# A new hand-out order for 959 planned operations, with the DMA queue chosen per transfer

## The chip, the cores and the metric

The kernel runs on one core of a Trainium2 chip. What counts is the device time of one execution in microseconds (us). The core has a matrix engine (PE, TensorE), a vector engine (DVE), an activation engine (ACT, ScalarE), a general engine (POOL, GpSimd) and a queue engine that only issues transfers (SP, SyncE). Transfers (DMA) can be issued from SP or from ACT; each engine works through its own list in order.

## The reference

Three stages follow each other, all in float32. (1) Linear attention with a decay per head: 2 batches, 8 heads, 768 positions, head size 64; `out = (q k^T * decay) v + q state`, with the state carried from block to block. (2) A dense layer: `x` (1536 x 512), `h = x @ w_in` (512 x 2048), `g = h * clip(h + 3, 0, 6) / 6`, `y = g @ w_out`. (3) A soft mixture of 8 experts: `logits = y @ phi` (32 slots); a softmax over all 1536 tokens mixes `y` into 32 slots; each expert runs `relu(slots @ w1) @ w2` (512 x 1024 x 512); a softmax over the slots mixes the experts' outputs back to 1536 x 512.

## The kernel before, in words

The sequence is cut into 12 pieces of 128 tokens (t = 0 to 11, six pairs tp). For a piece, attention is: transposes of q and k (`f_tr`, `f_tk`), scores (`f_sc`), decay (`f_pm`), state (`f_kd`, `f_pv`, `f_st`) and output (`f_px`). The decay table `dec` is loaded back from a small table that the kernel stores first (`store_pw`, `load_dec`). The dense layer is cut into 48 units `h_unit(t, n)` (n = 0 to 3, a quarter of w_in), each in two halves of six matmuls (L915): 96 halves in all, which serve below as a ruler along PE's list. After a unit, ACT (`f_u`, L929) and DVE (`f_g`, L935) make g, and both must be done before its PSUM buffer is free for a later unit. w_in is split into a high and a low part (`split_w_in`: ACT and DVE, some on POOL), which lets the three matmuls per tile stand for one float32 product.

`y` is never formed: phi is multiplied into w_out (`make_w2s`, giving `w2s`), and g into that (`f_lg`, L1019). Both need a blockwise transposition across partitions: DVE transposes 32 x 32 blocks (`f_blocks` L996, `f_wb` L670), and a *move* of four DMAs of 128 KB from SBUF to SBUF (`f_move` L1006 for g, `f_wq` L683 for w_out) brings the blocks to their partitions. For tp = 0 to 4 g goes this way, 5 x 4 = 20 moves; the last pair is transposed on PE. The softmax over tokens runs pair by pair (`f_lr`, `f_exp`, `f_pd`); after the last, the slots are formed (`f_psi`, L1312), spread for the experts (`f_sim`), and the experts' products follow (`f_p1` L1439, `f_po` L1473), then the outputs (`f_pt`, `f_ot`, `f_out`).

Expert weights (64 loads `e`) and the stored w_out (8 loads `wo`), 72 loads of 512 KB, are read on SP into a ring of 50 buffers of 4 KB per partition that everything shares, so a load waits until its buffer is given back.

The order of all this is written out by hand: `ORDER` names the 959 operations by the place at which the kernel creates them. `Plan.run` goes through it with a cost in ns for each operation, so as to know which ring buffer is free first, and thereby gives each operation its buffers; then it emits the operations. Before, it emits them sorted by the modelled start `t0`; a DMA's queue is fixed by kind: loads, stores of w_out (`sto`) and `f_wq` on SP (`mwq='SP'`), `f_move` on ACT (`mvq='ACT'`), the output stores in turn on SP and ACT (7 and 5). At the very start PE runs `lamq_products` and then `f_first`, eight products of a zero tile (`blank`), which compute nothing that is used.

Of the kernel before, what the change touches and what calls it, by code (L numbers as in the profile page):

```python
# [135 lines left out]
class Plan:  # L136
# [19 lines left out]

    def op(
        self, eng, cost, fn, deps=(), prio=0.0, take=(), rel=(), dma=0, reserve=None, follow=None,
        mode="F", lag=None, extra=0, share=2,
    ):  # L160
        o = Op()
        o.extra, o.share = extra, share
        o.lag = lag
        o.follow = follow
# [1458 lines left out]
```

## Time and profile before

| | |
|---|---|
| device time, median of 3 runs | 312.93 us (312.2 to 314.39) |
| profiled execution | 310.75 us, of it 309.0 us span |
| PE busy | 279.3 us (90%) |
| DVE busy | 195.8 us (63%) |
| ACT busy (issuing DMAs not counted) | 121.1 us (39%) |
| POOL busy | 38.0 us (12%) |
| DMA | 85.99 MB, mean 278 GB/s |

The span runs from the first to the last instruction; the rest of the profiled time lies around it. "Busy" leaves out waiting and the issuing of transfers. The granted clock of PE has two levels, 2.4 GHz (1.0) and 1.2 GHz (0.5). The median of the runs lies 2.18 us over the profiled execution.

### The profile page before, as it was taken

How to read it: one execution, taken by the hardware profiler on the slowest of the kernel's cores; microseconds unless marked ns; L12 is line 12 of the kernel's file. 1: busy time of each engine (PE TensorE's matmuls, PEld its weight loads, DVE VectorE, ACT ScalarE, POOL GpSimd, SP SyncE). 2: the span in 40 equal slices, each digit the busy share in tenths (PEclk: the TensorE clock that was granted, in tenths of full speed). 3: DMA queues.
4: the chain of work that ended last, by engine and by line, in shares of the span. 5: the costliest groups of instructions: out<-in, count | busy, mean ns of one | idle time of the engine just before them, and what ended most of it. 6: DMA issues, size and time to landing. Idle time of an engine off the chain costs nothing.

```text
span 309.0 us, 7097 instructions
## 1 busy us (share of the span) xinstructions
PE 279.3 (90%) x2854; PEld 215.9 (70%) x2854; DVE 195.8 (63%) x319; ACT 121.1 (39%) x227; POOL 38.0 (12%) x53
## 2 busy tenths in 40 slices
PE   4899999998999978999896999998999997889892
PEld 3877888786878856876775586865888655556671
DVE  5299979999989737778766659175464242430242
ACT  2566786997862530311303222221223520201141
POOL 5215013242400020002020020000000001000000
PEclk9999999999999995999999999999999999999996
DMA  7999999947799868585764579896998999999988
GB/s 183 295 330 290 337 323 359 299 149 229 222 276 284 255 190 214 158 232 164 200 157 117 137 240 297 259 319 223 366 395 286 369 421 416 418 417 415 350 274 265
DMA packets 80480, 85.99 MB, mean 278 GB/s; under 512 B 42040, under 2 KB 67136, under 8 KB 80448
## 3 DMA queue, kind: packets, MB, share of 16 engines
q1 hardware_dynamic: 67056, 73.75, 72.4%
q10 hardware_dynamic: 13392, 11.80, 13.3%
q8 instruction: 22, 0.36, 0.4%
q14 instruction: 10, 0.08, 0.1%
HBM read 64.55 MB, written 7.35 MB: 233 GB/s over the span
## 4 chain that ended last, share of the span: by engine, by line
PE 43%; DMA 18%; DVE 13%; ACT 9%; ACTq 7%; issue 4%; SPq 2%; POOL 1%; POOLq 0%; DVEq 0%
PE h L915 22%; DMA e<-in_moe_w_dram 12%; ACTq L1006 7%; PE pd L1134 3%; DMA gq<-gb 3%; PE lg L1019 3%; DMA wq<-wb 3%; ACT g L929 2%; DVE tmp_i L543 2%; DVE pm L797 2%; DVE tmp_i L550 1%; DVE g L935 1%; PE px L825 1%; ACT whi L576 1%; PE px L820 1%
## 5 line engine op out<-in xcount | busy, mean ns | idle before, releaser
L915 PE MATMUL h<-whi,x 128*128 128x512 f32 x384 | 122.9, 401 | 5.4 <-DVE g L935 4.8
L915 PEld LDWEIGHTS h<-whi,x 128*128 128x128 f32 x384 | 71.5, 191 | 24.9 <-DVE g L935 6.3
L915 PE MATMUL h<-wlo,x 128*128 128x512 f32 x192 | 75.7, 394 | 0.0
L929 ACT ACTIVATE g<-h,half_b 128x512 f32<-128x512 f32 x48 | 32.9, 689 | 70.8 <-PE h L915 39.9
L935 DVE SCALAR_TENSOR_TENSOR g<-g,h 128x512 f32<-128x512 f32 x48 | 32.6, 680 | 29.7 <-ACT g L929 29.3
L996 DVE STREAM_TRANSPOSE gb<-g 128x1024 f32<-128x1024 f32 x20 | 40.4, 2026 | 3.2 <-DMA gq<-gb 2.4
L915 PEld LDWEIGHTS h<-wlo,x 128*128 128x128 f32 x192 | 36.5, 190 | 8.0
L769 ACT COPY tr<-pt 128x512 f32<-128x512 f32 x24 | 13.3, 586 | 22.7 <-DMA gq<-gb 7.3
L843 POOL TENSOR_TENSOR states<-states,lamq 64x256 f32<-64x256 f32 x16 | 10.6, 660 | 65.9 <-DVE states L856 57.1
L778 POOL TENSOR_TENSOR vd<-qk,dec 128x512 f32<-128x512 f32 x10 | 11.4, 1145 | 57.6 <-DVE wo_f L550 25.9
L1439 PE MATMUL p<-e,sim 128*32 128x256 f32 x256 | 15.0, 380 | 3.4 <-DMA e<-in_moe_w_dram 2.1
L1473 PE MATMUL po<-e,ht 128*32 128x128 f32 (+1 forms) x384 | 16.1, 309 | 1.1 <-DMA e<-in_moe_w_dram 1.1
L797 DVE TENSOR_TENSOR pm<-ps,dec 128x512 f32<-128x512 f32 x24 | 15.6, 680 | 0.9 <-PE ps L789 0.7
L670 DVE STREAM_TRANSPOSE wb<-wo_f 128x1024 f32<-128x1024 f32 x6 | 12.1, 2012 | 6.2 <-DMA wq<-wb 6.2
L1458 DVE STREAM_TRANSPOSE ht<-hsi 128x256 f32<-128x256 f32 x8 | 4.9, 635 | 17.2 <-ACT hsi L1450 17.2
L789 PE MATMUL ps<-tr 64*128 64x128 f32 x192 | 14.5, 285 | 1.3 <-ACT tr L769 0.9
L550 DVE SCALAR_TENSOR_TENSOR tmp_i<-tmp_i 128x512 int32<-128x512 int32 x16 | 12.3, 780 | 5.1 <-ACT tmp_i L536 4.4
L789 PEld LDWEIGHTS ps<-tr 64*128 64x128 f32 x192 | 12.1, 187 | 4.9 <-issue 1.9
L1473 PEld LDWEIGHTS po<-e,ht 128*32 128x32 f32 x384 | 11.5, 110 | 5.3 <-DMA e<-in_moe_w_dram 1.6
L1439 PEld LDWEIGHTS p<-e,sim 128*32 128x32 f32 x256 | 8.0, 110 | 9.2 <-DMA e<-in_moe_w_dram 3.1
L832 ACT CAST x<-px 128x512 fp32r<-128x512 f32 x12 | 7.0, 585 | 18.3 <-DMA gq<-gb 8.7
L579 POOL TENSOR_TENSOR wlo<-tmp_i,whi 128x512 fp32r<-128x512 f32 x8 | 10.7, 1353 | 23.1 <-ACT whi L576 23.1
(117 smaller groups left out, 366.3 us busy)
## 6 DMA issues: line engine op xcount, KB each, us to landing
e<-in_moe_w_dram SPq DMA_DIRECT2D x64, 512.0 KB, 8.2
gq<-gb ACTq DMA_DIRECT2D x80, 128.0 KB, 3.4
wraw<-in_moe_w_in_dram SPq DMA_DIRECT2D x16, 512.0 KB, 5.8
wo_raw<-in_moe_w_out_dram SPq DMA_DIRECT2D x16, 512.0 KB, 5.4
wo_d<-wo_f SPq DMA_DIRECT2D x32, 128.0 KB, 3.2
wo<-wo_d SPq DMA_DIRECT2D x8, 512.0 KB, 6.9
qk<-in_k_dram SPq DMA_DIRECT2D x12, 256.0 KB, 5.8
qk<-in_q_dram SPq DMA_DIRECT2D x12, 256.0 KB, 4.7
```

The lines of the kernel that those rows point to most:

```text
L550: DVE.scalar_tensor_tensor(out=lw if dst is None else dst(), in0=hp, scalar=3, in1=lw, op0=ALU.logical_shift_left, op1=ALU.bitwise_or,)
L670: DVE.transpose(out=x.rearrange("p q d c f -> p c d q f"), in_=y.rearrange("p c (d t q) -> p c d q t", d=KT, q=4),)
L769: ACT.copy(T["tr", t][:, i], T["pt", t, i])
L789: PE.matmul(ps[g][:, p], lhsT=y[r, 1, p], rhs=y[r, 0, p], start=True, stop=True)
L797: DVE.tensor_tensor(out=T["pm", t].rearrange("p (a g) c -> p g a c", g=2)[:, g], in0=T["ps", t][g], in1=T["dec"].rearrange("p (a g) c -> p ...
L915: PE.matmul(ph, lhsT=xt[:, a, kt], rhs=T[w, n, part][:, kt % 2], start=i == 0, stop=i == 3 * KT - 1,)
L929: ACT.activation(T["g", tp, n][:, i], T["h", t, n], AF.Relu, bias=half_b, scale=1.0 / 6.0)
L935: DVE.scalar_tensor_tensor(out=to, in0=to, scalar=1.0, in1=T.pop(("h", t, n)), op0=ALU.min, op1=ALU.mult,)
L996: DVE.transpose(out=x.rearrange("p q c i t -> p i c q t"), in_=T["g", tp, n].rearrange("p i (c t q) -> p i c q t", c=4, q=4),)
L1006: QUEUE[CFG["mvq"]].dma_start(out=y[:, a].rearrange("p c i t -> p (c i t)"), in_=x[32 * a : 32 * a + 32].rearrange("f q c i t -> f (q c i ...
L1439: PE.matmul(p1[32 * j : 32 * j + 32], lhsT=T["sim"][:, e, b4], rhs=T["e1", e, b4][:, 256 * j : 256 * j + 256], start=b4 == 0, stop=b4 == 3,)
L1473: PE.matmul(T["po", hf][32 * qd : 32 * qd + 32], lhsT=T["ht", e // 4][:, e % 4, b8], rhs=T["e2", e, b8 // 2][:, b8 % 2, lo:hi] if e < WHOL ...
```

## The change

The list is replaced by another order of the same 959 operations; nothing is computed differently. Read through the operations' names, the two lists differ as follows where the prediction needs it ("at 42" is after 42 of the 96 halves on PE's list):

| on PE's list, or on a queue | before | after |
|---|---|---|
| first on PE | `lamq_products`, `f_first`, then piece 0's transposes | `f_first`, `lamq_products`, then piece 1's transposes |
| first loads on SP | w_in, k of pieces 1 and 0, `store_pw`, q 0, w_in, q 1, `dec` | k and q of piece 1, w_in, k 0, `store_pw`, q 0, w_in, q 2, `dec` |
| `f_sums` of n = 2, 3, 0 | at 26, 42, 46 | at 42, 42, 48 |
| `f_lg` of pairs 0, 1, 2 | at 52, 56, 64 | at 52 to 54, 60, 64 |
| `f_lg` of pair 3 | two at 68, two at 74 | all at 74 |
| `f_lg` of pair 4 | one at 78, three at 96 | two at 80, two at 96 |
| expert and wo loads listed ahead of `f_psi` | 46 | 45 |
| expert loads listed within the first 18 halves | none | two |
| g moves on ACT / on SP | 20 / 0 | 7 / 13 |
| most g moves on ACT with nothing between them | 3 (pair 2) | 1 (once with a store right behind it) |

Twelve operations in `BY_ACT` go to ACT, the other operations marked `free` to SP: of the 46 free ones these are seven g moves (402 is the store of w_out 13, 415 a `f_wq` of n = 0, 910, 934 and 955 are output stores). On SP's new list the moves of pairs 3 and 4 (n = 1, 3 and n = 0, 1, 3) stand between expert loads. `f_first` must now be done before `lamq_products`. The cost numbers of the model change, a move or load is modelled in its parts, and a part starts in the model only when the part eight before it has landed (`lanes`). Emission follows `ORDER` itself.

```diff
 ORDER = (
-    0, 74, 11, 256, 75, 4, 73, 3, 1, 5, 6, 76, 77, 78, 258, 257, 259, 10, 7, 89,
...
+    0, 1, 73, 74, 75, 4, 7, 89, 91, 10, 3, 92, 5, 6, 9, 14, 8, 2, 15, 90,
...
 )
+BY_ACT = (402, 415, 633, 639, 653, 679, 693, 699, 719, 910, 934, 955,)
...
-        dma_free, side, mode, shared = 0, 0, "F", 0
+        dma_free, side, mode, shared, lanes = 0, 0, "F", 0, [(0, 0)] * 8
...
             o = self.ops[i]
+            if o.free:
+                o.eng = "ACT" if i in BY_ACT else "SP"
...
+            for _ in range(o.parts):
+                now = max(now, lanes.pop(0)[0])
+                for t, _ in sorted(lanes):
+                    if o.rows / o.parts + sum(n for x, n in lanes if x - 900 > now) <= 200:
+                        break
+                    now = max(now, t - 900)
...
+                lanes.append((o.t1, o.rows / o.parts))
+                now += cost / o.parts
+                o.te = now
...
-        for i in sorted(ORDER, key=lambda i: self.ops[i].t0):
-            self.slots = self.ops[i].slots
+        for i in ORDER:
+            self.slots, self.eng = self.ops[i].slots, self.ops[i].eng
             self.ops[i].fn()
...
-    op("PE", 430 * CFG["fill"]["first"], f_first, [], -3000, take=[b_h], rel=[b_h])
+    ops["first"] = op("PE", 430 * CFG["fill"]["first"], f_first, [], -3000, take=[b_h], rel=[b_h])
...
-    ops["lamq_p"] = op("PE", 1150, lamq_products, deps=[pw_done], prio=-9, take=[b_x], rel=[b_pw])
+    ops["lamq_p"] = op("PE", 1700, lamq_products, deps=[pw_done, ops["first"]], prio=-9, take=[b_x], rel=[b_pw])
...
-                SP.dma_start(out=wo_d[c2, q4, n], in_=x[32 * q4 : 32 * q4 + 32])
+                QUEUE[plan.eng].dma_start(out=wo_d[c2, q4, n], in_=x[32 * q4 : 32 * q4 + 32])
...
-                    QUEUE[CFG["mwq"]].dma_start(
+                    QUEUE[plan.eng].dma_start(
...
-                QUEUE[CFG["mvq"]].dma_start(
+                QUEUE[plan.eng].dma_start(
...
-                (ACT if j % 2 else SP).dma_start(
+                QUEUE[plan.eng].dma_start(
```

## Rows read from the trace of the kernel before

**Rows 1.** The page, sections 1 and 2: busy time, and PE's clock in 40 slices

```profile
PE 279.3 (90%) x2854; PEld 215.9 (70%) x2854; DVE 195.8 (63%) x319; ACT 121.1 (39%) x227; POOL 38.0 (12%) x53
...
PEclk9999999999999995999999999999999999999996
```

**Rows 2.** Stretches: length, busy of PE, PEld, DVE, ACT, POOL, clock, DMA share, GB/s

```profile
15.00:105.00 90.00, 86.47 (x739) 71.69 (x738) 84.56 (x131) 66.35 (x113) 21.45 (x21) 1.00 0.90 282
105.00:165.00 60.00, 52.73 (x477) 41.03 (x476) 41.22 (x43) 12.97 (x22) 6.85 (x9) 0.94 0.71 188
165.00:240.00 75.00, 73.54 (x568) 55.08 (x567) 42.62 (x68) 19.44 (x41) 2.30 (x3) 1.00 0.82 266
240.00:299.00 59.00, 53.18 (x978) 35.83 (x978) 19.16 (x58) 14.26 (x37) 0.96 (x1) 1.00 1.00 387
```

**Rows 3.** Waits of PE, 105 to 256 us: total us, times, longest

```profile
PE h L915 <- DVE g L935: 3.2, 2, 2.5
PE w2p L695 <- DMA wq<-wb: 3.0, 2, 2.6
PE lg L1019 <- DMA gq<-gb: 1.5, 1, 1.5
PE lg L1019 <- ACT sm L1078: 1.0, 1, 1.0
```

**Rows 4.** Chain of waits, 129 to 216 us, shares by line

```profile
by line: PE h L915 26.3%; ACTq L1006 25.2%; DMA gq<-gb 8.5%; PE pd L1134 7.8%; PE lg L1019 7.5%; issue 2.7%; PE ps L789 2.5%; PE px L825 2.5%; DVE gb L996 2.3%; PE pv L810 2.1%; PE px L820 2.1%; PE pt L752 2.0%; PE lr L1089 2.0%; ACT g L929
```

**Rows 5.** Chain of waits, 250 to 309 us: shares by line, and one piece

```profile
by line: DMA e<-in_moe_w_dram 63.4%; PE pt L1542 5.2%; PE po L1473 5.0%; PE pd L1134 4.0%; PE keep_on L493 3.3%; PE p L1439 2.7%; PE psi L1312 1.6%; ACT ot L1557 1.0%; PE lg L1019 0.8%; PE pc L1408 0.8%; PE lr L1089 0.7%; ACT sm L1078 0.6%;
...
256.51 0.96 PE psi L1312 x33
```

**Rows 6.** PE's timeline at the start: start us, us, instruction, [idle before]

```profile
4.61 2.04 PE L481 MATMUL lamq_p<-pw,selp 32*128 32x128 f32 x8 [4.61 <-POOL low_rows L347]
6.58 3.78 PE L498 MATMUL first<-acc 128*128 128x128 f32 x16
...
18.03 1.09 PE L825 MATMUL px<-pm,vd 128*64 128x128 f32 x16
```

**Rows 7.** Timelines of DVE and POOL at the start

```profile
0.83 0.17 DVE L303 MEMSET acc<- 128x128 f32 x1 [0.83 <-PEq L1608]
...
13.06 2.08 POOL L778 TENSOR_TENSOR vd<-qk,dec 128x512 f32<-128x512 f32 x2 [7.45 <-DMA dec<-pw_d]
```

**Rows 8.** PE's timeline: its longest wait after the start

```profile
116.30 0.74 PE L695 MATMUL w2p<-wq,phi_b 128*32 128x64 f32 x4 [2.58 <-DMA wq<-wb]
```

**Rows 9.** Chain pieces: 24 matmuls of the dense layer, ahead of and behind that first wait

```profile
89.00 5.72 PE h L915 x24
...
118.49 7.75 PE h L915 x24
```

**Rows 10.** ACT's timeline ahead of PE's wait of 2.5 us for g

```profile
154.17 8.47 ACTq L1006 DMA_DIRECT2D gq<-gb  x12
162.68 0.58 ACT L832 CAST x<-px 128x512 fp32r<-128x512 f32 x1 [8.68 <-DMA gq<-gb]
```

**Rows 11.** The page, section 6: DMA issues, KB each, median us to landing

```profile
gq<-gb ACTq DMA_DIRECT2D x80, 128.0 KB, 3.4
...
wq<-wb SPq DMA_DIRECT2D x24, 128.0 KB, 2.6
```

**Rows 12.** DMA issues, 165 to 240 us

```profile
e<-in_moe_w_dram SPq DMA_DIRECT2D x26, 512.0 KB, 5.7
gq<-gb ACTq DMA_DIRECT2D x33, 128.0 KB, 4.6
```

**Rows 13.** Waits of SP's queue over the run: total us, times, longest

```profile
SPq L391 <- DMA gq<-gb: 24.3, 7, 15.6
```

**Rows 14.** Issue of moves on either queue: duration ns min/median/max, first and last start

```profile
L1006 ACTq DMA_DIRECT2D gq<-gb x80: 550/622/1651, 109.4 to 233.3; - x80
...
L683 SPq DMA_DIRECT2D wq<-wb x24: 542/604/1310, 79.9 to 125.4; - x24
```

More of the change, by code (lines that the diff above doesn't have):

```diff
@@ L158, in op @@
         self, eng, cost, fn, deps=(), prio=0.0, take=(), rel=(), dma=0, reserve=None, follow=None,
-        mode="F", lag=None, extra=0, share=2,
+        mode="F", lag=None, extra=0, share=2, parts=0, rows=8, free=False,
     ):
         o = Op()
-        o.extra, o.share = extra, share
+        o.extra, o.share, o.parts, o.rows, o.free = extra, share, parts, rows, free
         o.lag = lag
@@ L209, in run @@
                 shared = now + cost
-            o.t0, o.te, done[e] = now, now + cost, now + cost + o.extra
-            if o.dma and e == "ACT":
-                at = max(side, now + 400)
-                side = at + o.dma * (o.share if dma_free > at else 1)
-                dma_free = max(dma_free, at) + o.dma
-                o.t1 = side + self.DMA_TAIL
-            elif o.dma:
-                dma_free = max(dma_free, now + self.DMA_LEAD) + o.dma
-                o.t1 = dma_free + self.DMA_TAIL
-            else:
-                o.t1 = o.te + self.SETTLE[e]
+            o.t0, o.te = now, now + cost
+            o.t1 = o.te + self.SETTLE.get(e, 0)
+            for _ in range(o.parts):
[4 more added lines that the diff above has]
+                    now = max(now, t - 900)
+                if e == "ACT":
+                    at = max(side, now + self.DMA_LEAD)
+                    by = max(0, dma_free - at)
+                    size = o.dma / o.parts
+                    side = at + min(o.share * size, by + max(0, size - by / o.share))
+                    dma_free = max(dma_free, at) + size
+                    o.t1 = side + self.DMA_TAIL
+                else:
+                    dma_free = max(dma_free, now + self.DMA_LEAD) + o.dma / o.parts
+                    o.t1 = dma_free + self.DMA_TAIL
+                lanes.append((o.t1, o.rows / o.parts))
+                now += cost / o.parts
+                o.te = now
+            done[e] = o.te + o.extra
             for b in o.rel:
@@ L361, in load @@
     def load(
-        fn, nbytes, deps=(), take=(), rel=(), n=1, prio=None, reserve=None, eff=1.0, lag=None, eng="SP",
+        fn, nbytes, deps=(), take=(), rel=(), n=1, prio=None, reserve=None, eff=1.0, lag=None, eng="SP", share=2, each=440, rows=8, free=False,
     ):
         o = op(
-            eng, n * plan.DMA_ISSUE, fn, deps=deps, prio=-1000 if prio is None else prio,
+            eng, n * each, fn, deps=deps, prio=-1000 if prio is None else prio, share=share, parts=n, rows=rows, free=free,
             take=take, rel=rel, dma=nbytes / 360 / eff, reserve=reserve, lag=lag,
@@ L399, in load_qkv @@
         ops["ld" + x, t] = load(
-            fn, KB512 / 2, take=take, rel=[] if take else [bufs[name, t]], eff=0.61,
+            fn, KB512 / 2, take=take, rel=[] if take else [bufs[name, t]], eff=0.81, rows=64,
             reserve=load_reserve,
@@ L414, in load_w_in @@
         ops["ldw", n, kt] = load(
-            fn, KB512, take=[ring_buf(("wraw", n, kt))], reserve=load_reserve, eff=1.08
+            fn, KB512, take=[ring_buf(("wraw", n, kt))], reserve=load_reserve, eff=1.16
         )
@@ L426, in load_wo_raw @@
         ops["ldo", kk] = load(
-            fn, KB512, take=[ring_buf(("wo_raw", kk))], reserve=load_reserve, eff=1.08
+            fn, KB512, take=[ring_buf(("wo_raw", kk))], reserve=load_reserve, eff=1.16
         )
@@ L467, in attn_moe_softmoe_kernel @@
             ops["dec"] = load(
-                load_dec, KB512, deps=[ops["pw_d"]], take=[ring_buf("dec")], eff=0.5
+                load_dec, KB512, deps=[ops["pw_d"]], take=[ring_buf("dec")], eff=0.85, rows=64
             )
@@ L625, in convert_wo @@
                 store, KB512, [ops["cwo", kk], ops["cwo", kk - 1]],
-                rel=[bufs["wo_f", kk // 2]], n=4, prio=CFG["sto"], eff=0.7,
+                rel=[bufs["wo_f", kk // 2]], n=4, prio=CFG["sto"], eff=0.7, each=470, share=4, rows=8, free=True,
             )
@@ L707, in make_w2s @@
                 done.append(load(
-                    f_wq(h), KB512, [o], take=[b_t[h]], rel=[b_wb], n=4, eff=0.9, eng=CFG["mwq"],
+                    f_wq(h), KB512, [o], take=[b_t[h]], rel=[b_wb], n=4, eff=0.95, eng=CFG["mwq"], each=640, share=5, rows=32, free=True,
                     prio=CFG["mw"] if CFG["mwq"] == "SP" else prio - 1,
@@ L856, in f_st @@
                     DVE.tensor_tensor(out=dst, in0=dst, in1=T["pv", t][r], op=ALU.add)
-        tq = op("PE", 350, f_tr(0), [ops["ldq", t]], prio, take=[b_q], rel=[b_qk])
+        tq = op("PE", 425, f_tr(0), [ops["ldq", t]], prio, take=[b_q], rel=[b_qk])
         eq = op(
@@ L868, in attention @@
         tk = op(
-            "PE", 350, f_tk, [ops["ldk", t], tq], prio, take=[b_k] + x_k["take"], rel=[b_qk] + x_k["rel"],
+            "PE", 435, f_tk, [ops["ldk", t], tq], prio, take=[b_k] + x_k["take"], rel=[b_qk] + x_k["rel"],
             extra=x_k.get("extra", 0),
@@ L873, in attention @@
         ek = op("ACT", 480, f_ev(1), [tk, eq], prio, rel=[b_k])
-        sc = op("PE", 1090, f_sc, [eq, ek], prio, take=[b_s], rel=[b_tr], mode="T")
+        sc = op("PE", 1000, f_sc, [eq, ek], prio, take=[b_s], rel=[b_tr], mode="T")
         ops["sc", t] = sc
@@ L880, in attention @@
             kd = op(
-                "POOL", 1010, f_kd, [ops["ldk", t], ops["ldv", t], ops["dec"]], prio,
-                rel=[b_qk, bufs["dec"]],
+                "POOL", 1060, f_kd, [ops["ldk", t], ops["dec"], ops["ldv", t] if GREEDY else None], prio,
+                rel=[b_qk, b_vd, bufs["dec"]],
             )
@@ L885, in attention @@
                 sm = op(
-                    "POOL", 1160, f_sm, [prev, ops["px", t - 1], ops["lamq"], zeros], prio,
+                    "POOL", 1390, f_sm, [prev, ops["px", t - 1], ops["lamq"], zeros], prio,
                     rel=[bufs["lamq"]],
@@ L892, in attention @@
         px = op(
-            "PE", 1030 if c == 0 else 1920, f_px, [pm1, ops["ldv", t], trd, prev], prio - 0.1,
+            "PE", 940 if c == 0 else 1960, f_px, [pm1, ops["ldv", t], trd, prev], prio - 0.1,
             take=[b_x], rel=[b_vd, b_pm, b_states] + ([b_trd] if c > 0 else []),
@@ L1038, in logits @@
                 [o] + ([lgs[-CFG["depth"]] if len(lgs) >= CFG["depth"] else None] + w2s_all if GREEDY else []),
-                take=[b_last], rel=[b_gb], n=4, eff=0.9, eng=CFG["mvq"],
+                take=[b_last], rel=[b_gb], n=4, eff=1.0, eng=CFG["mvq"], each=660, share=5, rows=32, free=True,
                 prio=CFG["mv"] if CFG["mvq"] == "SP" else prio - CFG["mva"],
@@ L1055, in logits @@
         ops["lg", tp, n] = ops["lg"] = op(
-            "PE", 520, f_lg, [o, w2s_all[n], ops.get("lg") if GREEDY or not opens else None],
+            "PE", 440, f_lg, [o, w2s_all[n], ops.get("lg") if GREEDY or not opens else None],
             prio - 0.5,
@@ L1204, in attn_moe_softmoe_kernel, with load_b @@
     bprio = [100.0]
-    def load_b(key, fn, take, eff=1.15, nbytes=KB512):
+    def load_b(key, fn, take, eff=1.13, nbytes=KB512, rows=8):
         bprio[0] += 1
@@ L1209, in load_b @@
             fn, nbytes, [ops["ldv", NT - 1]] if GREEDY else [], take=take, prio=bprio[0], reserve=pre_reserve,
-            eff=eff, lag=CFG["lag"],
+            eff=eff, lag=CFG["lag"], rows=rows,
         )
@@ L1351, in attn_moe_softmoe_kernel @@
         o = op(
-            "PE", 872, f_psi(i), [o, ant[i // 2], ops["wo", 2 * i], ops["wo", 2 * i + 1]], 55,
+            "PE", 930, f_psi(i), [o, ant[i // 2], ops["wo", 2 * i], ops["wo", 2 * i + 1]], 55,
             take=[] if i else [b_x], mode="T",
@@ L1581, in combine @@
             ot[j].append(op(
-                "ACT" if g % 2 else "DVE", 550 if W < 512 else 600, f_ot(g), [o] + ot[j], pr,
+                "ACT" if g % 2 else "DVE", 610, f_ot(g), [o] + ot[j], pr,
                 take=[] if i else [b_o], rel=[b_h],
@@ L1587, in combine @@
                     f_out(j), 512 * NO * W, ot[j], rel=[b_o], prio=pr if j % 2 else 99,
-                    eff=0.95, eng="ACT" if j % 2 else "SP",
+                    eff=1.0, rows=16, free=True, eng="ACT" if j % 2 else "SP",
                 )
```

10 lines of the change are left out of this document (5 added, 5 removed), and 94 rows, old and new, of the table ORDER.

## The prediction

> **What bounds the kernel now.** I read the page first: PE is busy 279.3 of 309.0 us [rows 1], so an order can at most win the other 30 us, and PE's own work is the same afterwards. The stretches tell where those 30 us lie and what else is full there [rows 2]. From 15 to 105 us PE idles 90 - 86.5 = 3.5 us, and DVE is busy 84.6 of the 90: this part is nearly full on two engines. From 105 to 165 us PE idles 60 - 52.7 = 7.3 us with no engine full (DVE 41 of 60, DMA share 0.71): waits in a row of handovers, not throughput. From 165 to 240 us it idles 1.5 us. From 240 to 299 us the DMA share is 1.00 at 387 GB/s. The rest is the start: PE does nothing until 4.61 us [rows 6].
>
> Then the waits of PE from 105 to 256 us, four lines: 3.2 + 3.0 + 1.5 + 1.0 = 8.7 us [rows 3]. Who makes them is told by the chain of waits over 129 to 216 us: 25.2% of it, 22 us of 87, is ACT issuing the DMAs of the g moves at L1006, and 8.5% their flight [rows 4]. One DMA holds ACT 0.62 us, so 80 of them hold it 50 us [rows 14]. The place to look at is 154.17 us: twelve issues in a row, 8.47 us, and the copy of x behind them has waited 8.68 us [rows 10]; from there it goes on over DVE to the PE wait of 2.5 us for g [rows 3].
>
> The end hangs on transfers: of the chain from 250 us on, 63.4% is the flight of expert weights [rows 5]. Slots are formed at 256.51 us, and the list has 72 - 46 = 26 of the 72 loads still behind that point. At the rate of the stretch a load takes 524,288 B / 387 GB/s = 1.35 us [rows 2], 35 us for 26, and eight or so in flight come on top: the tail is a fixed length of DMA, counted from `f_psi`. So the time falls by as much as `f_psi` comes earlier, provided the loads keep their place in relation to PE.
>
> **The change part by part.** The sum is made on the profiled execution, 310.75 us (span 309.0); the median of the runs is 2.18 us above it, and I shift the sum by that.
>
> *Zero products first.* They need only the blank tile, cleared at 1.00 us [rows 7], and take 3.78 us [rows 6]; now they stand behind `lamq_products`, which begins at 4.61 us. In the new order they lie inside that idle time: `lamq_products` ends at 6.65 us as before, and the transposes, which now begin when the zero products end, may begin up to 3.7 us earlier. What is late next is the decay table: POOL's first use of it waits until 13.06 us [rows 7], and the new list puts one more load of 256 KB ahead of it (0.93 us at 282 GB/s [rows 2]), so about 14.0 us. The first output product stands at 18.03 us now [rows 6], 5 us behind the table; DVE's new list does the two decay products ahead of the first low part of w_in (`f_lo`), the old one behind it, so the distance shrinks, while the table comes later. I take -2.0, the middle; bounds -3.7 (all of it) and 0 (table or conversion holds it).
>
> *15 to 105 us.* DVE has 5.4 us of idle, PE 3.5 [rows 2]; reordering can't thin out their work. I take -0.5, between -2.9 (most of PE's idle gone) and +2.5: two expert loads now come within the first 18 halves, where the DMA share is 0.90, and may push the conversion loads back by 2 x 1.35 us.
>
> *The sums of w2s.* `f_sums` of n = 2 moves from 26 to 42 on PE's list, that of n = 3 stays at 42 behind it, n = 0 goes from 46 to 48. The waits on `wq` are 3.0 us [rows 3]. Behind the long one of 2.58 us [rows 8] PE's clock stands at the half level: the clock of its slice is 0.5 [rows 1], and 24 matmuls take 7.75 us where 24 before took 5.72 [rows 9], which is 2.0 us. With three sums close together and more slack ahead of the first, I take all of it, -5.0; bounds -5.0 and 0, since n = 3 has not been given more room.
>
> *Moves off ACT.* Thirteen of 20 go to SP; one `wq` move and one store come to ACT, so ACT loses (52 - 8) x 0.62 = 27 us of issuing, nearly all between 109 and 233 us [rows 14]. No more than one move stands before ACT's next copy (once with a store behind: 8 issues, 5 us), where it was three. The waits for g, 3.2 us [rows 3], go: -3.2, bounds -3.2 and 0. On SP, an issue is as long (0.60 us [rows 14]); the 52 issues there cost 31 us of a queue that mostly waits for buffers: 24.3 us in one line alone [rows 13]. While SP waits for a block to be transposed, the loads behind it wait too.
>
> These rows say the gain lies in ACT's time. The Trainium skill says as much against any other gain: "DMA: Bandwidth & Descriptors", section "Issuing engines are not separate DMA queues", holds that transfers of all issuing engines share the same 16 DMA engines and that spreading them saves only the time of issuing, which is usually small beside the DMA. The trace agrees on the first; on "small" it differs, four issues being 2.5 us beside 3.4 us to landing [rows 11, 14]. By the rule's "small" this term would be about zero and the time 3.2 us longer than mine.
>
> *New waits.* The logits keep their two waits, 1.5 and 1.0 us [rows 3], as I see no more room for them on balance (pair 1 goes from 56 to 60, but the second of pair 4 comes from 96 to 80). Some handover that is covered now will not be: I add the same again, +2.4. Bounds 0 and +5.2, twice the longest wait seen.
>
> *Tail.* 45 loads ahead of `f_psi` instead of 46, and the same five loads last: 0, bounds one load, 1.35 us, either way. Which engine issues the output stores, the new buffers and the model's cost numbers: 0, since the last stores are again two small ones on either queue, and buffers matter only through the waits counted above.
>
> Sum: -2.0 - 0.5 - 5.0 - 3.2 + 2.4 = -8.3 us. Nearly all of it lies ahead of 165 us, where the DMA has room (share 0.71); everything behind moves forward as it is. Profiled 302.4, median **304.6 us**. All bounds together: 16 us less, or 9 us more.
>
> **Rivals.** *The gain is taken back ahead of `f_psi`.* The start holds at the decay table, and the waits of the middle only change places: DVE is nearly full to 105 us, and four pairs of logits now come later, closer to each other. Against it: the middle has no full engine. Then -2.0 (start) -0.5 +1.0 or so: about 311.4, within 309.8 and 316.
>
> *SP's queue becomes the bound (slower).* Place: the moves of pairs 3 and 4, which now stand on SP between expert loads that wait for buffers. SP's longest wait is 15.6 us [rows 13]. If such a one lies ahead of a move, `f_lg` waits for it; a move at the right moment would have gone out from ACT. Behind two halves of cover (2 x 6 matmuls of 0.24 us, 2.9 us) some 12.7 us stay, plus 2.0 us for the half clock [rows 9]: -8.3 + 14.7 = +6.4, so 319.3 us. From a wait of 9.2 us on (8.3 + 2.9 - 2.0) the gain is gone, from 12.3 us on the kernel is slower by 1%. Also a move sent out behind loads lands later: loads take 5.7 us there, moves on their own queue 4.6 [rows 12], while `wq` on a quiet SP took 2.6 [rows 11]; that adds 1.1 us. Beside it, the Trainium skill ("DMA: Bandwidth & Descriptors", "Queues, rings and completion order") has each DMA engine take turns between the issuing queues' rows, which would favour a move on ACT's own row; no row here separates the two. For it: rows 13. Against it: two of pair 4's moves feed logits that stand at 96, with 16 halves of room, and from 240 us on (share 1.00) loads queue up anyway.
>
> *The change does not do what it says.* If the first matmul waits for something later than the blank tile, the zero products don't move into the idle time: 2.0 us more than mine, 306.6. It lies within the range.
>
> **Numbers.** A single comparison tells about 1% (3.1 us) from no change. The forecast case, own range 299.5 to 309.8: 0.62. More than that (a tail with fewer waits too): 0.05. The first rival: 0.18. The slower one: 0.15. Faster 0.67, same 0.18, slower 0.15. The range leaves 0.05 below and 0.15 above: 299.5 to 315.
>
> **What would show it.** Right: the first matmul at about 1 us and `px` of the first piece near 16 us (18.03 now); no slice of PE's clock below 1.0 between 20 and 290 us; ACT's issues at L1006 28 instead of 80, with no run of more than four, and their share of the chain from 129 to 216 us under a half of 25%; PE's idle time between 105 and 165 us under 4 us; `f_psi` near 248 us and 52 us from there to the end. Wrong: `f_psi` early but the tail longer than 55 us (loads held back on SP); waits of `f_lg` on `gq` of more than 4 us in sum; or new PE waits before 105 us of more than 4 us.

## The result and the profile after

The new kernel takes 298.87 us (median of 4 runs, 298.24 to 299.67); the kernel before, run beside it, 313.66 us (312.2 to 323.22). The ratio is 0.9544, 95% interval 0.9492 to 0.9597. The direction was forecast, the size was not: 304.6 us lies 5.7 us too high, and the time is 0.6 us below the range's low end. Here and below the ratios leave out runs in which the chip was in a slower state (over 1.5% above the kernel's fastest), the medians have them in, and the profile of e1 is of such a run.

The profiled execution of the new kernel took 299.16 us (span 297.4), against 310.75 (309.0). So from profile to profile 11.6 us went, where the sum had 8.3. The other 2.5 us of the miss are no event in the kernel: I added 2.18 us for the distance from profile to median, and the new kernel's profiled run stands 0.3 us above its median instead of 2.18 below.

The page of the new kernel, sections 1 and 2, answers to [rows 1]:

```profile
PE 275.9 (93%) x2854; PEld 213.3 (72%) x2854; DVE 195.7 (66%) x319; ACT 121.0 (41%) x227; POOL 38.1 (13%) x53
...
PEclk9999999999999999999999999999999996999998
```

The low clock slice in the middle is gone, and there is another one at 245 us, in the tail. Busy time of the other engines is the same. The stretches of [rows 2] in the new kernel (same columns):

```profile
15.00:105.00 90.00, 86.58 (x677) 71.30 (x672) 79.76 (x125) 66.04 (x113) 22.08 (x21) 1.00 0.93 287
105.00:165.00 60.00, 57.58 (x649) 44.34 (x651) 46.14 (x54) 15.50 (x30) 7.24 (x10) 1.00 0.75 197
165.00:240.00 75.00, 74.87 (x591) 54.55 (x582) 42.60 (x64) 21.57 (x44) 2.28 (x3) 1.00 0.91 311
240.00:299.00 59.00, 46.24 (x873) 33.46 (x872) 18.87 (x56) 10.55 (x28) 0.96 (x1) 0.91 0.97 364
```

PE's idle time between 105 and 165 us fell from 7.3 to 2.4 us, and it ran 649 matmuls there instead of 477.

Stretches of the clock don't hold the same work in both kernels. Two marks do: the end of `f_sums` of n = 3 (909 matmuls lie ahead of it in either kernel) and the start of `f_psi` (with the small product `f_rt` just ahead of it). The stretches of the kernel before, cut at these marks (columns as above):

```profile
0.00:118.49 118.49, 106.48 (x909) 88.70 (x909) 95.29 (x154) 76.61 (x130) 30.14 (x43) 0.99 0.88 268
118.49:256.34 137.85, 131.92 (x1128) 98.23 (x1130) 85.23 (x126) 34.52 (x72) 7.64 (x10) 0.98 0.80 255
256.34:309.00 52.66, 40.94 (x827) 29.02 (x826) 15.23 (x41) 9.94 (x25) 0.20 (x1) 0.95 0.97 363
```

And of the kernel after:

```profile
0.00:111.84 111.84, 103.29 (x909) 85.90 (x909) 93.06 (x153) 75.86 (x129) 30.25 (x43) 1.00 0.92 277
111.84:243.79 131.95, 129.68 (x1117) 96.19 (x1117) 85.61 (x118) 35.39 (x74) 6.91 (x9) 1.00 0.84 266
243.79:297.40 53.61, 42.97 (x831) 31.24 (x830) 17.07 (x50) 9.76 (x24) 0.96 (x1) 0.91 0.99 371
```

| stretch | before | after | measured | by my terms |
|---|---|---|---|---|
| to the end of `f_sums` n = 3 | 118.49 | 111.84 | -6.65 (idle -3.5, busy -3.2) | -2.0 - 0.5 - 3.0 = -5.5 |
| from there to `f_psi` | 137.85 | 131.95 | -5.90 (idle -3.7, busy -2.2) | -2.0 - 3.2 + 2.4 = -2.8 |
| from `f_psi` to the end | 52.66 | 53.61 | +0.95 | 0 |

(The -5.0 of the sums is split here: 3.0 us of waits ahead of the first mark, 2.0 us of half clock behind it.) The larger part of the miss is in the second line: 3.1 us more than my terms have. (Two profiles can differ without a cause: in e6 below, whose edit changes nothing in the time, `f_psi` begins at 258.5 us instead of 256.4. So single lines of one to two us are no proof by themselves.)

PE's waits from 105 us to `f_psi`, whole answer, to be laid beside [rows 3]:

```profile
PE pv L824 <- ACT tr L783: 1.6, 1, 1.6
PE w2p L709 <- DVE w2s L678: 0.8, 1, 0.8
PE pd L1148 <- DVE sm L1129: 0.5, 1, 0.5
```

All four lines of before are gone, the two of the logits as well, and 2.9 us stand where 8.7 were. The chain of waits from 129 to 216 us [rows 4] is now work on PE alone; ACT's issuing, 25.2% of it before, isn't in it:

```profile
by line: PE h L929 60.1%; PE lg L1033 9.9%; PE pd L1148 8.2%; PE ps L803 5.5%; PE px L839 4.7%; PE px L834 4.1%; PE pt L766 3.0%; PE pv L824 2.1%; PE lr L1103 2.0%; PE lr L1098 0.8%
```

PE's timeline at the start, the answer to [rows 6]:

```profile
1.05 3.75 PE L512 MATMUL first<-acc 128*128 128x128 f32 x16 [1.05 <-DVE acc L317]
...
11.79 0.63 PE L766 MATMUL pt<-ident,qk 128*128 128x128 f32 x4 [1.20 <-DMA qk<-in_q_dram]
...
14.75 0.69 PE L824 MATMUL pv<-vd 128*64 128x64 f32 x16 [1.24 <-POOL vd L792]
...
17.04 1.09 PE L839 MATMUL px<-pm,vd 128*64 128x128 f32 x16
```

The zero products moved into the idle time as forecast; PE then waits for q and for the decay table, and `px` comes 1.0 us earlier in this profile (18.03 before). That is not firm: in the eight profiles with this first list (this one, e1, e5, e8, e9, e10, e14, e15) `px` begins anywhere from 16.75 to 19.15 us.

The moves themselves, by queue (durations in ns, as in [rows 14]):

```profile
L1020 SPq DMA_DIRECT2D gq<-gb x52: 542/602/769, 117.6 to 224.6; - x52
L1020 ACTq DMA_DIRECT2D gq<-gb x28: 550/622/1299, 110.0 to 213.0; - x28
```

Their time to landing from 165 to 240 us (median us in the last column, as in [rows 12]):

```profile
gq<-gb SPq DMA_DIRECT2D x20, 128.0 KB, 4.1
gq<-gb ACTq DMA_DIRECT2D x12, 128.0 KB, 6.4
```

And two of the waits of SP's queue, over the run, beside [rows 13]:

```profile
SPq L1020 <- DMA gq<-gb: 14.8, 11, 3.6
SPq L405 <- DMA gq<-gb: 6.6, 3, 4.2
```

The 15.6 us wait of the SP queue, on which the slower rival rested, shrank to 4.2. In the tail, PE's timeline shows `f_psi` stopping for a load of w_out:

```profile
243.87 0.62 PE L1326 MATMUL psi<-wo,ant 128*32 128x128 f32 x16
247.83 6.15 PE L1326 MATMUL psi<-wo,ant 128*32 128x128 f32 x112 [3.33 <-DMA wo<-wo_d]
```

112 matmuls take 6.15 us behind that wait; the granted clock from 247.8 to 254 us is 0.52, the 1.2 GHz level. In this profile the chain that ended last, from 238 us on, lies mostly on PE and on that wait:

```profile
by line: PE p L1453 23.8%; PE po L1487 17.0%; DMA wo<-wo_d 16.2%; DMA e<-in_moe_w_dram 12.0%; PE psi L1326 10.5%; PE pt L1556 5.0%; PE pc L1422 2.7%; DVE ot L1571 1.2%; DVE hsi L1346 0.7%; ACT hsi L1338 0.6%; issue 0.6%; SPq L1231 0.5%; PE 
```

The same kernel in another profile (e14 below) waited 2.70 us at this place and kept the full clock:

```profile
246.38 3.27 PE L1326 MATMUL psi<-wo,ant 128*32 128x128 f32 x112 [2.70 <-DMA wo<-wo_d]
```

There `f_psi` is done 4.3 us earlier, the chain from 240 us on is expert loads, and the span is 296.8 instead of 297.4 us:

```profile
by line: DMA e<-in_moe_w_dram 83.7%; PE pt L1556 5.2%; PE po L1487 3.3%; DVE ot L1571 1.2%; PE pr L1530 0.5%; issue 0.5%; SPq L1242 0.1%; SPq L1252 0.0%
```

So PE's work and the loads are nearly of one length in the new tail: the half clock put PE into the chain and moved the end little.

### The profile page after: what moved, and what is told of

Same layout as the page of the kernel before. It is cut to its first block, busy times and chain, and to the rows that moved or that the text cites. A ratio compares the mean times of both kernels' runs of the same rounds, so it can differ in the third digit from the quotient of the medians.

```text
span 297.4 us, 7102 instructions
## 1 busy us (share of the span) xinstructions
PE 275.9 (93%) x2854; PEld 213.3 (72%) x2854; DVE 195.7 (66%) x319; ACT 121.0 (41%) x227; POOL 38.1 (13%) x53
## 4 chain that ended last, share of the span: by engine, by line
PE 70%; DMA 15%; DVE 7%; SPq 2%; issue 2%; ACT 1%; ACTq 1%; POOL 0%; DVEq 0%
PE h L929 36%; PE p L1453 5%; PE lg L1033 4%; PE po L1487 3%; DMA wo<-wo_d 3%; PE px L839 3%; PE pd L1148 3%; PE ps L803 3%; PE px L834 2%; DMA e<-in_moe_w_dram 2%; PE psi L1326 2%; PE pt L766 2%; DMA qk<-in_q_dram 2%; DMA qk<-in_k_dram 2%; PE pv L824 2%
## 5 line engine op out<-in xcount | busy, mean ns | idle before, releaser
L929 PE MATMUL h<-whi,x 128*128 128x512 f32 x384 | 121.4, 397 | 0.3 <-DVE g L949 0.2
L929 PEld LDWEIGHTS h<-whi,x 128*128 128x128 f32 x384 | 70.1, 188 | 18.7 <-DVE g L949 2.1
L792 POOL TENSOR_TENSOR vd<-qk,dec 128x512 f32<-128x512 f32 x10 | 10.6, 1062 | 56.7 <-PE h L929 24.0
L766 PE MATMUL pt<-ident,qk 128*128 128x128 f32 x96 | 13.3, 276 | 4.6 <-DMA qk<-in_q_dram 4.3
L766 PEld LDWEIGHTS pt<-ident,qk 128*128 128x128 f32 x96 | 10.8, 140 | 6.9 <-ACT tr L783 2.4
L564 DVE SCALAR_TENSOR_TENSOR wo_f<-tmp_o 128x512 int32<-128x512 int32 x16 | 12.0, 758 | 4.6 <-DMA wq<-wb 2.3
L543 ACT ACTIVATE tmp_i<-wraw 128x512 f32<-128x512 f32 x16 | 11.0, 684 | 6.5 <-DMA wraw<-in_moe_w_in_dram 6.5
```

The source lines that it names most:

```text
L564: DVE.scalar_tensor_tensor(out=lw if dst is None else dst(), in0=hp, scalar=3, in1=lw, op0=ALU.logical_shift_left, op1=ALU.bitwise_or,)
L766: PE.transpose(p[:, a], x[:, i, 2 * a : 2 * a + 2].rearrange("p a d -> p (a d)"), ident,)
L929: PE.matmul(ph, lhsT=xt[:, a, kt], rhs=T[w, n, part][:, kt % 2], start=i == 0, stop=i == 3 * KT - 1,)
```

## The experiments

"Old" is the kernel before with one edit, "new" the changed kernel with one edit. Each ratio is to the kernel before, run in the same group; its median was 314.26, 313.73, 313.78 and 314.09 us in the four groups.

**Moves back on ACT (e1), new list.**

```diff
-                QUEUE[plan.eng].dma_start(
+                ACT.dma_start(
```

> The new order with all 20 g moves issued by ACT again; order, buffers and all else as in the new kernel. Theory A (a good part of the gain is ACT's freed time): the 13 moves put 52 x 0.62 = 32 us of issuing back on ACT, the waits of PE for g return, 3 us or more, about 302 to 304 us. Rival B (the order alone does it; where the moves are issued is indifferent): 298.9 within 1 us. Rival C (SP is the worse place, moves stand behind loads there): faster, 297.

307.91 us (304.37 to 309.34), ratio 0.9763 [0.9672, 0.9854]. Of the gain of 4.6% the list keeps 2.4% with the moves on ACT; the queue is worth the rest, 2.2% (1.6% against e14 below, the same new kernel in a later group): 5 to 7 us by the ratios. That is more than the 3.2 us of waits for g that I could see before, though against e14 the intervals reach down to some 1.6 us. PE's waits from 105 to 255 us begin:

```profile
PE ps L803 <- ACT tr L783: 2.6, 2, 1.4
PE pg L992 <- ACT gt L1000: 1.9, 1, 1.9
PE px L834 <- DVE x L850: 1.9, 1, 1.9
PE pv L824 <- ACT tr L783: 1.0, 1, 1.0
```

and ACT's timeline has the picture of [rows 10] again, in the new list:

```profile
154.27 9.76 ACTq L1020 DMA_DIRECT2D gq<-gb  x12
164.07 0.59 ACT L846 CAST x<-px 128x512 fp32r<-128x512 f32 x1 [9.25 <-DMA gq<-gb]
```

Only 0.5 us of PE's waits there are for g, and none is one of the logits. Three lines, 5.5 us, are at the small steps of attention (`tr` and x), whose ACT work stands behind the issues. The 1.9 us of the last transposition are another matter: they come at 239.8 us, when ACT has made its last issue by 230.6 us and its g has waited 5.4 us for an expert load.

**Moves on SP in the old list (e2).** Seven moves stay on ACT, the other thirteen go to SP.

```diff
-                QUEUE[CFG["mvq"]].dma_start(
+                (ACT if (tp, n) in ON_ACT else SP).dma_start(
```

> The old order with the same 13 moves issued by SP that the new kernel issues there; all else as before. Theory A: the waits of PE for g behind ACT's issues go, 3 us of 313.7, so about 310, and the wait of 2.6 us on wq with its half clock stays. Rival B: no change, 313.7 within 1.5 us. Rival C (a list not made for it: SP stands at a move while loads wait behind it): 316 or more.

311.49 us (309.55 to 314.43), ratio 0.9941 [0.99, 0.9982]. The waits for g behind 105 us are gone, and `f_psi` starts at 253.38 instead of 256.36, 3.0 us earlier: near the -3.2 of my term (with 2 us of scatter between profiles, as e6 shows). In this profile nothing of it arrives at the end (span 310.8 against 309.0 us), and over the runs 0.6% does. PE's timeline in `f_psi`:

```profile
260.52 1.08 PE L1313 MATMUL psi<-wo,ant 128*32 128x128 f32 x16 [5.64 <-DMA wo<-wo_d]
```

The last w_out loads aren't there yet, and the tail is 57.4 us instead of 52.7. Queue alone 0.6% and order alone 2.4% make 3.0%; both together gave 4.6% (4.0% in a later group, e14). That the two help each other is suggested by this, not shown: the intervals allow a plain sum.

**The w_out loads first, in that list (e12).** As e2, with two `wo` loads moved ahead of six expert loads in the list.

```diff
 ORDER = (
...
-    742, 717, 743, 745, 720, 723, 737, 614, 615, 739, 767, 814, 809, 724, 785, 725, 611, 738, 736, 780,
+    742, 717, 743, 745, 720, 723, 737, 614, 615, 739, 767, 765, 766, 724, 814, 725, 611, 738, 736, 809,
```

> The old order with 13 moves on SP, as tried before (311.5; slots began 3.0 us earlier than before, but psi then waited 5.9 us for stored w_out and the clock fell), now with the last two loads of the stored w_out ahead of six expert loads. Theory (the 3 us won on PE were lost in these waits): 308 to 309. Rival D (the tail has a fixed length of DMA whatever psi waits for): 311 within 1 us.

312.2 us (310.3 to 313.9), ratio 0.9957 [0.9921, 0.9993]: no more than e2. `f_psi` runs through (128 matmuls in 3.68 us), and the wait turns up at the experts; the first of PE's waits from 105 us on:

```profile
PE p L1440 <- DMA e<-in_moe_w_dram: 5.8, 2, 4.2
```

**The same in the new list (e5).** Four `wo` loads change places with expert loads.

```diff
 ORDER = (
...
-    595, 711, 596, 597, 598, 846, 608, 609, 821, 610, 774, 733, 735, 780, 770, 795, 599, 612, 613, 789,
+    595, 711, 596, 597, 598, 846, 608, 609, 821, 610, 774, 733, 735, 767, 770, 762, 599, 612, 613, 766,
```

> The new kernel with the last four loads of the stored w_out (5, 0, 4, 1) put ahead of six expert loads of the same size on SP's list; each list place keeps its buffer. The 3.3 us wait of psi and the half clock behind it (psi's last 112 matmuls take 6.2 us, at full clock about 3.7) should go, so the experts begin some 5 us earlier. Theory D (the tail has a fixed length of DMA): the last expert load still lands about 287 us, so at most 1.5 us are won, 297.4 to 298.9. Rival (the tail is bound by PE): 4 to 5.5 us, 293.5 to 295.

300.98 us (300.07 to 301.33), ratio 0.9656 [0.9615, 0.9697]: no gain. `f_psi` ends at 249.7 instead of 254.0, and the tail is 54.4 us. The chain from 240 to 299 us:

```profile
by line: DMA e<-in_moe_w_dram 81.7%; PE pt L1556 5.1%; PE po L1487 3.3%; DVE ot L1571 1.2%; PE pr L1530 0.5%; issue 0.5%; SPq L1242 0.1%; SPq L1252 0.0%
```

The expert loads that gave up their places come later here, so e5 alone can't say what the wait cost; together with e14, where the list is unchanged, it says that the 3.3 us wait and the half clock in the new tail cost next to nothing. In both lists taking a PE wait out of the tail leaves its length, as a tail made of DMA would. It is not fixed, though, when counted from `f_psi`: e2 began `f_psi` 3.0 us earlier, loads in their old places, and its tail grew by 4.7 us.

**Zero products first, in the old list (e3), and undone in the new (e13).** In e13 `lamq_products` comes first and no longer depends on `f_first`.

```diff
 ORDER = (
-    0, 74, 11, 256, 75, 4, 73, 3, 1, 5, 6, 76, 77, 78, 258, 257, 259, 10, 7, 89,
+    0, 73, 74, 11, 256, 75, 4, 3, 1, 5, 6, 76, 77, 78, 258, 257, 259, 10, 7, 89,
```

> The old order with only the zero products put ahead of lamq_products on PE. Theory A: PE's first transposes begin up to 3.7 us earlier, but the decay table still comes at 13 us, so the end moves by -1 to -2 us, about 312. Rival B: nothing, since the first pieces of the dense layer wait for the conversion of w_in and the table, 313.7 within 1 us.

> The new kernel with lamq_products put back ahead of the zero products on PE's list. By my prediction's term the start is worth 2.0 us, by the after-trace (first output product at 17.0 and not 18.0) 1.0: 300 to 301. Rival (PE's start is not what the first pieces wait for, the decay table is): 299 within 0.7 us.

e3: 311.47 us (309.76 to 314.68), ratio 0.9896 [0.9826, 0.9966]; `px` starts at 16.37 (17.70 to 18.11 in the other profiles of the old list), `f_psi` at 255.28 (-1.1, within scatter). e13: 300.28 us (297.81 to 301.33), ratio 0.9599 [0.9537, 0.9661]; the unchanged new kernel in the same group (e14) 0.9599 [0.953, 0.9668]. In the old list the step is worth about 1%; in the new one nothing that these runs can tell, although PE then waits 4.6 us for POOL's first constants as before [rows 6] and `px` begins at 19.24 us.

**Sums later in the old list (e4).** `f_sums` of n = 3 goes from 42 to 46 halves, so that `wq` has time to land.

```diff
 ORDER = (
...
-    171, 62, 414, 586, 587, 415, 178, 438, 642, 439, 179, 180, 588, 589, 444, 445, 446, 590, 412, 413,
-    655, 188, 191, 447, 181, 189, 638, 184, 348, 416, 185, 417, 580, 656, 639, 581, 582, 591, 186, 544,
+    171, 62, 414, 586, 587, 415, 178, 642, 179, 180, 588, 589, 444, 445, 438, 446, 590, 412, 413, 655,
+    188, 191, 447, 439, 181, 189, 638, 184, 348, 416, 185, 417, 580, 656, 639, 581, 582, 591, 186, 544,
```

> The old order with f_sums of n = 3 moved on PE's list from behind 42 halves to behind 46. Theory A (the wait on wq and the half clock behind it cost 3.0 us and what the slow matmuls lose): by my prediction's 2.0 us for the clock 308.7; by the after-trace, where the dense layer's matmuls are 2.2 us and the w2s products 2.0 us shorter in sum, 306.5. Rival B (the wait only passes to the next sums or to the logits): 312 to 314.

319.24 us (318.69 to 324.0), ratio 1.0155 [1.0097, 1.0213]: slower, which neither side expected. The wait for `wq` is mostly gone (1.4 us from 75 to 170 us), but PE now waits 8.8 us for g there. The chain of waits around the longest one:

```profile
115.53 3.73 DMA gq<-gb
...
119.29 0.05 DVEq L797
...
119.61 0.66 DVE g L935
```

DVE's queue stands at L797 (`f_pm`) until a g move has landed, and g comes behind it. The plan tells why: the later sums give two ring buffers back later, so `f_pm` of piece 7 is handed one that this move must release first. A place in the list is also a place in the ring of buffers, and a step that is moved for one wait makes another elsewhere.

**Keeping the clock up in the old list (e7).** Sixteen matmuls of the identity stand inside `f_sums` of n = 3; their output is not used.

```diff
             for h in range(2):
+                for _ in range(16 if n == 3 and h == 1 else 0):
+                    PE.matmul(p[:, 64:128], lhsT=ident, rhs=ident[:, 0:64], start=True, stop=True)
```

> The old order with 16 matmuls that compute nothing in the middle of f_sums of n = 3, where PE waits 2.58 us for wq, so that PE is not idle there. If they keep the clock at its upper level, they cost nothing and give back what the half clock costs: 2.0 us by my prediction (312), about 4 us by the after-trace, where the dense layer's and the w2s products are 4.2 us shorter in sum (310). Rival: the PE time won is lost again at the next wait for g, 313.7.

318.2 us (314.94 to 319.71), ratio 1.0176 [1.0045, 1.0307]. The clock stays at its full level from 105 to 165 us (0.94 before), and the next output product on PE comes 1.39 us earlier (125.57 against 126.96). That is the larger part of the 2.0 us of my term. It is lost at the next handovers, PE's waits from 105 to 262 us:

```profile
PE lg L1021 <- DMA gq<-gb: 4.2, 2, 3.2
PE h L917 <- DVE g L937: 2.5, 2, 2.2
```

`f_psi` begins at 259.4 us, 3.0 later than before. Why the kernel is slower, and not only no faster, these rows don't settle.

**Emission in the list's order (e6), old list.**

```diff
-        for i in sorted(ORDER, key=lambda i: self.ops[i].t0):
+        for i in ORDER:
```

> The old order, emitted as the list stands and not sorted by the modelled start; each engine's own order is the same. Theory: nothing but the emission changes, so the time is that of before within 1%, 311 to 316. Rival (the emission order ties SP's and ACT's transfers together and carries part of the gain): 3 us or more faster, 310 or less.

313.08 us (310.53 to 322.19), ratio 1.0015 [0.9964, 1.0066]: no effect.

**ACT's time by itself (e8, e10), new list.** Where a move goes out on SP, ACT makes ten useless copies of about 0.32 us in its place (e10: five). DMAs and SP's list stay as they are.

```diff
+            for _ in range(10 if plan.eng == "SP" else 0):
+                ACT.copy(dump, ident[:, 0:120])
```

> The new kernel, its 13 moves issued on SP, but ACT does ten small copies that nothing uses at the list place of each of the 13 moves, so that ACT loses about the time that issuing would take there, without standing at the move and waiting for its block or buffer. Theory A (ACT's issuing time is what costs): like the kernel with all moves on ACT, 303 to 308. Rival E (what costs is that ACT stands at a move until its block and its buffer are ready, with its other work behind): near 299, at most 301.

> The new kernel with five copies that nothing uses on ACT at each of the 13 moves (1.6 us each, 21 us in sum; ten were 42 us and gave 312). Theory A with a time on ACT that pays in proportion: 298.9 + 21/42 x 13 = 305. Rival (there is slack on ACT, and only long blocks cost, since two moves often follow each other): 300 to 302.

e8: 312.05 us (310.06 to 313.95), ratio 0.9992 [0.9949, 1.0036]: the whole gain is gone, with no DMA changed. The filling, 42 us, is longer than the 32 us of issuing in whose place it stands, so this shows that time on ACT is what costs, not how much of the gain it was. e10: 301.34 us (300.18 to 304.07), ratio 0.9626 [0.9563, 0.969]. ACT's timeline in e8 has copies where issues stood before [rows 10]:

```profile
156.99 6.46 ACT L1026 CAST dump<-ident 128x120 f16<-128x120 f32 x20
```

and PE's waits from 105 to 256 us begin with two lines of e1, those behind ACT's `tr` and x:

```profile
PE ps L804 <- ACT tr L784: 4.8, 2, 2.7
PE px L835 <- DVE x L851: 2.1, 1, 2.1
```

**All moves on SP (e9; again as e15, beside the unchanged new kernel, e14).**

```diff
-                QUEUE[plan.eng].dma_start(
+                SP.dma_start(
```

> The new kernel with all 20 g moves issued by SP, none by ACT. Theory A (ACT's freed time is what pays): 28 more issues, 17 us, leave ACT; 13 moves gave 9 us of 308, so the other seven may give 0 to 3 us, 296 to 299. Rival C (SP's list is then the bound: loads wait behind moves that wait for their block): slower, 301 or more, with SP's waits at the line of the moves above 20 us and a longer tail.

> The new kernel with all 20 g moves on SP once more, for its interval: if the seven moves left on ACT still cost, 297 and 1 to 2 us below the new kernel of the same call; if the first look was chance, the same as that.

> The new kernel once more, unchanged, beside the next one on the same chip: 298 to 300.

e9: 297.21 us (295.84 to 299.39), ratio 0.9505 [0.9441, 0.957]. e15: 295.47 us (294.32 to 298.71), ratio 0.9467 [0.9402, 0.9532]; beside it e14 with 301.07 us (297.39 to 303.57), ratio 0.9599 [0.953, 0.9668]. This is the fastest version: 0.4% below the changed kernel in e9, which the intervals don't separate, and 1.3% (4 us) below it in one group, e15 against e14, where they only touch. PE's waits from 105 us to `f_psi` in e9, whole answer:

```profile
PE w2p L709 <- DVE w2s L678: 0.8, 1, 0.8
PE pd L1148 <- DVE sm L1129: 0.5, 1, 0.5
```

The 1.6 us wait for ACT is gone as well, and the clock has no low slice in the tail. Put in a row by what ACT has to do for the thirteen moves or instead of them:

| ACT's time against the changed kernel | median us | ratio |
|---|---|---|
| -17 us (e9, e15: 28 issues fewer, 0.62 us each) | 297.21, 295.47 | 0.9505, 0.9467 |
| 0 (the changed kernel, e14) | 298.87, 301.07 | 0.9544, 0.9599 |
| +21 us (e10: 65 copies) | 301.34 | 0.9626 |
| +32 us (e1: 52 issues) | 307.91 | 0.9763 |
| +42 us (e8: 130 copies) | 312.05 | 0.9992 |

The first 21 us cost little, the next 21 cost 10.7 us, half of their length. Either ACT's idle time takes most of the first 21 us in, or only long blocks cost (each move's copies hold ACT 1.6 us in e10 and 3.2 us in e8). These runs don't tell the two apart.

**Both q and k of the first pieces first (e11), new list.** The aim was the 1.2 us waits for q at the start.

```diff
 ORDER = (
-    0, 1, 73, 74, 75, 4, 7, 89, 91, 10, 3, 92, 5, 6, 9, 14, 8, 2, 15, 90,
+    0, 1, 73, 74, 75, 4, 7, 89, 91, 3, 6, 92, 10, 5, 8, 9, 14, 2, 15, 90,
```

> The new kernel with the first loads in another order: k and q of pieces 1 and 0, then w_in, the store and the load of the decay table, and then the second w_in and q of piece 2. The table has 0.75 MB less ahead of it and q of piece 0 does not stand behind the store, so PE's first waits (0.8, 1.2 and 1.2 us) shrink and the first output product comes near 15.5 us, not 17.0. Theory F (the start hangs on the table): 1 to 1.5 us faster, 297.5. Rival (the start hangs on the conversion of w_in, which now comes later): 299 to 300.

302.17 us (300.46 to 305.56), ratio 0.9622 [0.9558, 0.9686]: not faster, and `px` begins at 22.10 us. PE's waits for q, up to `f_psi`, are 5.1 us with one of 4.1 (4.3 us with none over 1.2 in the changed kernel):

```profile
PE pt L766 <- DMA qk<-in_q_dram: 5.1, 3, 4.1
```

because of a wait of SP's queue within the first 20 us, 0.7 us in the changed kernel:

```profile
SPq L458 <- DMA pw_d<-rp: 4.1, 1, 4.1
```

The load of the decay table waits for its store, and the third q load now stands behind it on SP.

## Why the prediction was right in direction and short in size

**What bounds the kernel: right in the main.** A row of handovers in the middle, with ACT's issuing as what holds them up, and a tail that is a length of DMA. e8 shows the first without touching a transfer; e5, e12 and e14 bear out the second. That the time falls by as much as `f_psi` comes earlier held for the change (12.5 us earlier, 11.6 us less) and not for e2.

**Start: -2.0 expected, -1.0 read** at `px`, and that within the scatter of the new list's start; the fastest profile, e15, has `px` at 19.07. The table was what is late next, as said, and a wait for q came with it. In the old list the step gave about 1% (e3), in the new one nothing measurable (e13). That the first stretch still comes out near my terms (-6.65 against -5.5) is partly luck: the start gave less, the sums more.

**15 to 105 us: -0.5 expected.** PE's idle time there went from 3.5 to 3.4 us. The waits for g ahead of 105 us fell from 1.6 to 0.2 us, and 2.3 us of waits for q took their place.

**Sums of w2s: -5.0 expected, somewhat more measured.** The waits for `wq` ahead of the mark, 3.4 us, became one of 0.8 us for `w2s`. PE's busy time fell by 3.2 us ahead of the mark and by 2.2 behind it, for all but the same matmuls. I had counted the half clock at 2.0 us, from 24 matmuls of the dense layer; the small matmuls of the sums (5.3 us busy before, 3.3 after) and `lamq_products` (2.04 before [rows 6], 1.15 after) take less as well, and these rows don't tell how much of that is the clock. With 2.2 us less for the dense layer, 2.0 for the sums' matmuls and 2.6 less of waiting it is 6.8 us. Alone in the old list neither the wait (e4) nor the clock (e7) can be cashed in; e4 moved buffers as well, so it is no clean test.

**Moves off ACT: -3.2 expected.** In the old list about that arrived at `f_psi` (e2: -3.0), and in the new list the waits for g are gone. But inside the new list the queue is worth 5 to 7 us (e1), because the issues hold up not only g: copies of transposes and of x on ACT stand behind them. The prediction drew on the Trainium skill, "DMA: Bandwidth & Descriptors", section "Issuing engines are not separate DMA queues", for the view that the saving of issue time is usually small. The runs here fit that what is saved is issue time (e8 costs the gain with the DMAs unchanged) and not that it is small: 32 us of issuing on an engine that is 41% busy cost 5 to 7 us. That both queues share the DMA engines, with which the prediction says the trace agrees, is only how the profile counts their packets (72.4% for SP's and 13.3% for ACT's queue of the same 16 engines' time before); no run tests it.

**New waits: +2.4 expected, -0.4 measured. This is the step that failed, in its first half: that the logits keep their waits.** I wrote that I saw no more room for the logits, kept their 2.5 us of waits, and added "the same again" for covers that would go. Behind the first mark PE waits 2.1 us in all (1.6 for ACT, 0.5 for DVE; 1.5 us in e14). So new waits of about the size did come, by luck, since the +2.4 named no handover; but the logits' 2.5 us are gone: 2.1 - 2.5 = -0.4. That is 2.8 of the 3.1 us by which the second stretch beat my terms, 2.5 of them the logits'. PE's timeline of before has their two waits:

```profile
153.47 1.93 PE L1019 MATMUL lg<-gq,w2s 128*32 128x256 f32 x32 [0.96 <-ACT sm L1078]
214.04 0.64 PE L1019 MATMUL lg<-gq,w2s 128*32 128x256 f32 x8 [1.46 <-DMA gq<-gb]
```

They stand at pair 1 and at the first of pair 4, and just these two places come later in the new list, from 56 to 60 and from 78 to 80 halves. I had weighed the first against pair 4's second and passed over pair 4's first. The room comes from the order and not from the queue: with the new list and all moves on ACT the logits wait for nothing (e1), with the old list and the moves on SP they still wait 2.9 us for g moves (e2). The covers that I feared for, 5.5 us in three lines of e1, are lost when ACT issues the moves, and that is what the change took away.

**Tail: 0 expected, +0.95 measured**, 53.6 us where I said 52. `f_psi` came at 243.9, not 248; it then waited 3.3 us for w_out and ran at the low clock, which put PE's work into the last chain; without the low clock the loads end it at nearly the same time (e14, e5).

**The rivals.** Gain taken back ahead of `f_psi` (311.4): no, PE's idle time is lower in both stretches. SP's queue as the bound (319.3): no. The moves on SP landed in 4.1 us from 165 to 240 us, those on ACT in 6.4, and SP's wait of 15.6 us shrank to 4.2; e9 with all moves on SP is faster still. That the zero products don't move: they did, at 1.05 us.

**The signs I named.** Kept: first matmul at 1.05 us; 28 issues on ACT, never more than four in a row; its share of the chain under half of 25% (none); PE idle 2.4 us, under 4, between 105 and 165 us; `f_lg` on `gq` under 4 us (none); tail under 55 us. Not kept: `px` near 16 (17.04), no slice of the clock below 1.0 (one at 245 us), `f_psi` near 248 us (243.9). And one sign of being wrong came up: new PE waits before 105 us of more than 4 us. They are 4.3 us for q and 1.2 us for the table. They cost nothing in sum, since the 4.6 us wait at the very start [rows 6] went to 1.05 us.

**The base.** Shifting both kernels by the distance that one profile has from its median cost 2.5 us of the 5.7. It should have been in the range rather than in the sum.

Open: which steps of the new order make the 2.4% that it is worth without the queue (single steps in the old list, e3, e4 and e7, don't add up to it), why e7 is slower than before, what e11 lost beyond its first wait, and whether queue and order really give more together than apart.

## What to carry to other kernels

Where a busy engine waits in a row of handovers, add up the issuing that a compute engine does for DMAs ahead of its own work, even when that engine is 40% busy, and price it by all the work behind the issues, not by the waits that happen to name it; a wait, kept or new, goes into a sum only with the handover at which it stands. One wait taken out of a tight list, or one step moved, is mostly lost at the next handover (e2, e7, e12) or, through shared buffers, costs more than it brings (e4). Where the tail is a length of DMA, taking a PE wait out of it gave nothing (e5, e12); that loads which begin earlier would help is argued, not shown.

## What the runs showed of the hardware that was not expected

- A DMA of 128 KB from SBUF to SBUF holds SP as long as ACT (0.602 and 0.622 us), but the moves on the busier SP queue landed sooner than those on ACT: 4.1 against 6.4 us from 165 to 240 us. They went out at different moments, so this is no comparison of the queues by themselves.
- In the kernel before, PE's wait of 2.58 us at 116 us was followed by the low level of its clock, the one of 2.5 us for g [rows 3] by none (granted clock 1.00 from 160 to 170 us). In e7 useless matmuls in the first wait kept the clock at 1.0, and the kernel got no faster by it.
- `f_psi` at the low level took 6.15 us for 112 matmuls in one profile of the changed kernel, and 3.27 us at the full clock in another (e14), behind waits of 3.33 and 2.70 us. The end came at nearly the same time (297.4 and 296.8 us).
